# First batch of a retention and Fourier-mixing kernel: k transposed straight from f32 on TensorE, its decay moved into the masked eviction, loads and weight issues reordered

## The chip, the cores and the metric

The kernel runs on one core of one Trainium2 chip. The metric is the device time of one execution in microseconds (us). Before the change it is 247.43 us, the median of three runs (247.37 to 247.91). The profiled execution has a span of 246.0 us. Engines are named as in the profile: PE is TensorE (PEld its weight loads), DVE is VectorE, ACT is ScalarE, POOL is GpSimd, SP is SyncE, whose queue issues the loads and stores.

## The reference

Inputs are q, k and v of shape [4 batches, 8 heads, 768 positions, 64], and two weight matrices of 512 x 2048 and 2048 x 512, all f32. The first part is retention with a decay gamma for each head, gamma = 1 - 2^(-5-h). For each position t it updates a 64 x 64 state and reads it out:

```
state = gamma * state + outer(k[t], v[t])
y[t]  = (1/8) * q[t] @ state
```

The eight heads side by side give x of shape [4, 768, 512]. The second part adds to x the real part of its two-dimensional Fourier transform over positions and channels (u), normalises each row of u to mean 0 and variance 1 (un), and returns

```
u + relu(un @ w_ch1) @ w_ch2
```

## The kernel before

**Tiling of the retention.** A batch's 768 positions are cut into 6 chunks of 128 (NCH), its 8 heads into 4 pairs, taken in the order 0, 1, 3, 2 (PAIR_ORDER). Inside a chunk the sum over earlier positions is a matrix product: scores k q^T, masked to the causal triangle and weighted with powers of gamma, times v. Across chunks a state is carried. For a pair the kernel makes:

- q16: q cast to f16 (q0_unit, L388, on Pool), and kd: k cast to f16 and multiplied with gamma^(127-p), p being the position in the chunk (k0_unit, L396, on Pool; for the last pair the second head is on ScalarE, L408).
- qT and kT: both transposed on TensorE, six 128x128 transposes each (t0_unit, L424), through a PSUM tile that ScalarE copies to SBUF (te_unit, L436). Since kT comes from kd, the decay of k is already in the scores.
- the scores of the two heads, 12 small matmuls (am_unit, L447), which VectorE multiplies with the causal mask and with the constant gamma^(-128) while it moves them out of PSUM to atm (ae_unit, L462). This is the masked eviction. Four of them make a pair.
- the state product kd^T v of five chunks (kv0_unit, L471, needs kd and v16) and the scan over chunks on VectorE (sc_unit, L484), which reads the factors of gamma^128 from gk5. gk5 is filled per pair by gk_unit (L223) on ScalarE, from gk2.
- y: the state read with q (yx_unit, L509) and atm times v (yi_unit, L495), moved to x by ScalarE with the factor gamma^(p+1)/8 (x0_unit, L525).

**The Fourier part and the layer.** Tables of sines and cosines are worked out on the chip at the start (trig_dve, L277, on VectorE; t_act, L308, on ScalarE); x is folded (fold_s, fold_d on VectorE) and multiplied with them (s1_unit, s2_unit). The two layers are the matmuls of L930, L947 and L973, which fill TensorE from about 40 us to the end.

**Order of the work.** The first batch is written out by hand in first_units (L1031): a list of units, each of which emits a few instructions. After each unit pin() fixes the order on every engine, so that an engine takes its instructions in the order of this list. Between the units stand fillers (L142): 128x512 matmuls of zeros that only keep TensorE at work, six of them before the first unit, then four, three, one and so on. From the second batch on, units are spread by due times in several streams (emit).

**Loads.** The loads of the first batch are issued at the start on SP's queue, in the order q, k, v of pair 0, then of pair 1 and so on, 384 KB each (load_unit, L152); k's load takes both heads of the pair. The weights come later in eight pieces of 512 KB from Pool's queue (w1_unit, w2_unit): w1_unit(0) stands in the list just after the cast of pair 3's q, the other seven after the cast of its v.

**PSUM.** The transposes, the scores and the state product share a pool of five banks (ps_g), given out in turn.

Of the kernel before, what the change touches and what calls it, by code (L numbers as in the profile page):

```python
# [11 lines left out]
AF = mybir.ActivationFunctionType  # L12
# [6 lines left out]
P = 128  # L19
# [18 lines left out]
def kernel(  # L38
# [113 lines left out]
    def load_unit(b, i, after=None):  # L152
        def run():
            h0 = 2 * PAIR_ORDER[i]
            for name, src in srcs.items():
# [3 lines left out]
                dma = nc.sync.dma_start(t, src[b, h0:h0 + 2].rearrange(rows, p=P))  # L159
# [21 lines left out]
    gexp = const.tile([P, 2, H], f32, tag="gexp")  # L181
    gq8, gkd = gexp[:, 0], gexp[:, 1]
    ident16 = const.tile([P, P], f16, tag="ident16")
    tmp = up.tile([P, NCH, DM], f32, tag="u32", name="tmp")
# [13 lines left out]
    for h in range(H):  # L198
# [6 lines left out]
                            op0=ALU.mult)  # L205
    nc.scalar.activation(gexp, gexp, AF.Exp, bias=0.0, scale=1.0)
# [4 lines left out]
    make_identity(nc, ident16)  # L211
    nc.gpsimd.affine_select(out=maskf, in_=maskf, compare_op=ALU.is_ge, fill=0.0, base=0,
# [10 lines left out]
    def gk_unit(hp):  # L223
        def run():
            nc.scalar.copy(gk5[:, hp, :, 1:], gk2[:, hp:hp + 1].unsqueeze(1).to_broadcast(
                [P, D, NCH - 2]))
        return run
# [168 lines left out]
    def k0_unit(i):  # L396
        def run():
            h0 = 2 * PAIR_ORDER[i]
            k32 = in_of.pop(("k", 0, i))
            kd = kd_of[0, i] = kp.tile([P, NCH, 2, D], f16, tag="kd16", name="kd16")  # L400
            nc.gpsimd.tensor_scalar(out=kd[:, :, 0, :], in0=k32[:, 0], scalar1=gkd[:, h0:h0 + 1],
                                    scalar2=1.0, op0=ALU.mult, op1=ALU.mult)
            if i < 3:
                nc.gpsimd.tensor_scalar(out=kd[:, :, 1, :], in0=k32[:, 1],
                                        scalar1=gkd[:, h0 + 1:h0 + 2], scalar2=1.0,
                                        op0=ALU.mult, op1=ALU.mult)
            else:
                nc.scalar.activation(kd[:, :, 1, :], k32[:, 1], AF.Copy, bias=0.0,  # L408
                                     scale=gkd[:, h0 + 1:h0 + 2])
        return run  # L410
# [13 lines left out]
    def t0_unit(i, part):  # L424
        def run():
            if part == 0:
                at[0, i] = dict(kT=tp.tile([P, NCH, P], f16, tag="kT", name="kT"),
                                qT=qts[i % 2][:, 0])
            src = (q16_of, kd_of)[part][0, i]
            tq = at[0, i]["tq", part] = ps_g.tile([P, NCH, P], f16, tag="g", name="tq",  # L430
                                                  padded_shape=[P, 8, P])
            for c in range(NCH):
                nc.tensor.transpose(tq[:, c, :], src[:, c].rearrange("p a b -> p (a b)"), ident16)
        return run

    def te_unit(i, part):  # L436
        def run():
            st = at[0, i]
            tq = st["tq", part]
            if part == 0:  # L440
                nc.scalar.copy(st["qT"].rearrange("p c t -> p (c t)").rearrange(
                    "p (t c) -> p t c", c=NCH), tq.rearrange("p c t -> p t c"))
            else:
                nc.scalar.copy(st["kT"], tq)
        return run
# [16 lines left out]
    def ae_unit(i, half, h2):  # L462
        def run():
# [3 lines left out]
                scalar=float(gam[2 * PAIR_ORDER[i] + h2] ** (-P)),  # L467
# [516 lines left out]
    def w1_unit(g):  # L984
        def run():
            f0 = g * (DFF // 4)
            w_dma.append(nc.gpsimd.dma_start(
                w116[:, :, f0:f0 + DFF // 4],
                moe_w_ch1[:, f0:f0 + DFF // 4].rearrange("(cb p) f -> p cb f", p=P)))
        return run  # L990
# [40 lines left out]
    def first_units():  # L1031
# [10 lines left out]
        def x(i):  # L1042
# [5 lines left out]
        un = [ts_dve(0), gk_unit(o[0]), gk_unit(o[1]), t_act(0, 0), t_act(0, 1),  # L1048
              q0_unit(0), t0_unit(0, 0), filler(4), ts_dve(1), te_unit(0, 0), t_act(0, 2),
              k0_unit(0), t0_unit(0, 1), filler(3), te_unit(0, 1), ts_dve(2), td_dve(0), t_act(1, 0),  # L1050
              t_act(1, 1), t_act(1, 2), v0_unit(0)]
        un += a(0) + [filler(1), kv0_unit(0)] + e(0, *std) + [sc_unit(0)]
        un += [q0_unit(1), t0_unit(1, 0), te_unit(1, 0), t_act(2, 0), t_act(2, 1), filler(4),
               k0_unit(1), t0_unit(1, 1), te_unit(1, 1)]
# [3 lines left out]
        un += [q0_unit(2), t0_unit(2, 0), te_unit(2, 0), csn_unit(1), filler(3), k0_unit(2),  # L1058
               t0_unit(2, 1), te_unit(2, 1)]
        un += y(1) + [td_dve(1), yx_unit(1), filler(2)] + x(1) + [  # L1060
            gk_unit(o[2]), t_act(3, 0), t_act(3, 1), v0_unit(2)]
        un += a(2) + [filler(1), kv0_unit(2)] + e(2, *std) + [sc_unit(2), t_act(3, 2),
                                                              csn_unit(2)]
        un += [q0_unit(3), w1_unit(0), t0_unit(3, 0), te_unit(3, 0), filler(3)] + y(2)
        un += [fold_s(0, 0, 258, 0, 1), g0_unit(0, (0,)), k0_unit(3), t0_unit(3, 1),
               te_unit(3, 1), yx_unit(2), gk_unit(o[3]), x0_unit(2, 0), x0_unit(2, 1),
               t_act(4, 0), t_act(4, 1), filler(2), v0_unit(3)]
        un += [w1_unit(g) for g in range(1, 4)] + [w2_unit(g) for g in range(4)]
        un += a(3) + e(3, (0, 0), (1, 0)) + [kv0_unit(3), filler(4), sc_unit(3), t_act(4, 2)]
# [108 lines left out]
```

## Time and profile before

Busy time of the whole span and of the first 30 us, from the profile:

| engine | busy in the span, us | 0 to 10 us | 10 to 20 us | 20 to 30 us |
|---|---|---|---|---|
| PE | 234.4 (95%) | 7.31 | 8.66 | 7.98 |
| DVE | 177.5 (72%) | 8.77 | 9.36 | 8.94 |
| ACT | 124.3 (51%) | 8.14 | 8.85 | 7.34 |
| POOL | 81.3 (33%) | 7.11 | 5.59 | 8.39 |

A row of a timeline gives the start and the duration in us, then the engine, the line, the operation, what is written and read, the shape and the number of instructions; in brackets stands how long the engine was idle before it and what ended that. Rows merge neighbours, so that the duration of "x6" is that of all six together. A row of the waits gives the total in us, how often, and the longest. In a table by stretches each engine has its busy time and the number of its instructions.

The loads of the first batch land, from issue and time to landing, at 4.2, 6.0 and 7.7 us (q, k, v of pair 0), 8.9, 10.7, 12.4 (pair 1), 13.4, 15.3, 17.0 (pair 2) and 19.6, 21.3, 22.6 us (pair 3).

### The profile page before, as it was taken

The page shows a single profiled execution, that of the slowest core. Times are in us where ns is not written, and L with a number is a line of the kernel's source. Part 1 is how long each engine was busy: PE and PEld are TensorE (multiplying, and loading weights), DVE is VectorE, ACT ScalarE, POOL GpSimd, SP SyncE. Part 2 cuts the span into 40 slices and gives each one's busy share as a digit, 9 for nine tenths or more (in the row PEclk, how much of TensorE's full clock was granted, in tenths as well). Part 3 has the DMA queues.
Part 4 walks back from the last instruction along what each step waited for, and adds up shares of the span by engine and source line. Part 5 has one row for each costly group of instructions (what it writes and reads, how often), then busy time and mean ns, then how long its engine had stood idle before and what let it go on. Part 6 is the DMA issues. An engine that isn't in the chain of part 4 may idle for free.

```text
span 246.0 us, 5309 instructions
## 1 busy us (share of the span) xinstructions
PE 234.4 (95%) x2024; PEld 144.4 (59%) x2024; DVE 177.5 (72%) x430; ACT 124.3 (51%) x276; POOL 81.3 (33%) x146
## 2 busy tenths in 40 slices
PE   6897899999999999999999999999999998999994
PEld 2454668956676655665567446665666455445543
DVE  8998957898788788995987648887895657424122
ACT  8798669477785445742247415732257217202500
POOL 6667600376500068690001637660003214000000
PEclk9999999999999999999999999999999999999999
DMA  8998999699999287988999589596100331121012
GB/s 174 257 260 138 200 204 206 152 250 261 275 233 214 56 171 176 190 174 149 242 266 210 119 183 181 108 138 150 58 0 3 60 133 30 38 85 43 0 45 85
DMA packets 99209, 36.39 MB, mean 148 GB/s; under 512 B 89840, under 2 KB 96240, under 8 KB 99184
## 3 DMA queue, kind: packets, MB, share of 16 engines
q1 hardware_dynamic: 94960, 31.86, 62.5%
q0 software_dynamic: 4224, 4.19, 10.5%
q8 instruction: 16, 0.26, 0.5%
q14 instruction: 9, 0.07, 0.1%
HBM read 27.26 MB, written 6.29 MB: 136 GB/s over the span
## 4 chain that ended last, share of the span: by engine, by line
PE 72%; DVE 8%; POOL 7%; ACT 4%; SPq 3%; DMA 2%; issue 2%; POOLq 0%; DVEq 0%
PE psc L973 30%; PE psh L930 23%; SPq L159 3%; PE ps L730 3%; PE psh L947 3%; PE wkA L594 3%; DMA k<-in_k_dram 2%; PE wkY L648 2%; POOL u L864 2%; POOL u L866 2%; PE wkY L644 1%; DVE bst L883 1%; PE wkK L613 1%; DVE u L834 1%; PE pq L827 1%
## 5 line engine op out<-in xcount | busy, mean ns | idle before, releaser
L973 PE MATMUL psc<-w,ht 128*128 128x512 f16 (+1 forms) x400 | 89.6, 370 | 0.1
L930 PE MATMUL psh<-unT,w 128*128 128x384 f16 x448 | 81.3, 326 | 0.6 <-ACT ht L934 0.6
L973 PEld LDWEIGHTS <-ht 128*128 128x128 f16 x400 | 38.1, 98 | 35.5 <-issue 0.3
L930 PEld LDWEIGHTS <-w 128*128 128x128 f16 x448 | 42.3, 98 | 24.9 <-issue 1.3
L934 ACT ACTIVATE ht<-psh 128x384 f16<-128x384 f32 x64 | 30.6, 488 | 39.4 <-PE psh L930 38.3
L864 POOL TENSOR_TENSOR u<-u,x 128x256 f32<-128x256 f32 x21 | 13.3, 634 | 102.3 <-DVE u L834 90.7
L977 DVE SCALAR_TENSOR_TENSOR ob<-psc,stats,u 128x512 f32<-128x512 f32 (+1 forms) x25 | 18.1, 722 | 27.4 <-PE psc L973 27.3
L936 DVE TENSOR_SCALAR ht<-psh 128x384 f16<-128x384 f32 x48 | 26.3, 551 | 8.6 <-PE psh L930 8.3
L597 DVE TENSOR_TENSOR atm<-wkA,maskp 128x512 f16<-128x512 f32 x36 | 23.9, 685 | 1.0 <-PE wkA L594 1.0
L885 ACT ACTIVATE un<-u,stats 128x512 f16<-128x512 f32 x21 | 15.1, 721 | 16.9 <-DVE stats L884 8.7
L883 DVE BATCH_NORM_STATS2 bst<-u 128x6 f32<-128x512 f32 x21 | 14.6, 694 | 9.7 <-POOL u L866 9.5
L623 DVE SCALAR_TENSOR_TENSOR s<-s,gk,wkK 128x128 f16<-128x128 f16 x48 | 16.4, 343 | 2.3 <-ACT s L619 1.4
L656 ACT ACTIVATE x<-wkY,gexp 128x384 f16<-128x384 f32 x24 | 12.8, 580 | 9.3 <-PE wkY L648 9.3
L145 PE MATMUL wps<-ht 128*128 128x512 f16 x40 | 13.3, 439 | 2.2 <-POOL ht L196 2.2
L377 POOL TENSOR_SCALAR kd<-k,gexp 128x384 f16<-128x384 f32 x24 | 13.8, 584 | 2.4 <-DMA k<-in_k_dram 2.4
L866 POOL TENSOR_TENSOR u<-u,x 128x256 f32<-128x256 f32 x21 | 13.3, 634 | 2.8 <-DVE u L837 1.5
L594 PE MATMUL wkA<-qTz,kT 128*128 128x256 f16 x72 | 13.6, 273 | 0.0
L829 ACT COPY qn<-pq 128x128 f32<-128x128 f32 x18 | 4.9, 274 | 14.1 <-PE pq L827 13.9
L947 PE MATMUL psh<-unT,w 128*128 128x128 f16 x192 | 11.5, 219 | 0.1
L947 PEld LDWEIGHTS <-w 128*128 128x128 f16 x192 | 11.0, 98 | 0.7 <-issue 0.5
L382 POOL TENSOR_SCALAR v<-v 128x768 f16<-128x768 f32 x12 | 10.0, 830 | 2.0 <-DMA v<-in_v_dram 1.9
L594 PEld LDWEIGHTS <-kT 128*128 128x128 f16 x72 | 6.9, 98 | 6.0 <-DVE s L623 0.4
(164 smaller groups left out, 318.2 us busy)
## 6 DMA issues: line engine op xcount, KB each, us to landing
q<-in_q_dram SPq DMA_DIRECT2D x16, 384.0 KB, 6.2
k<-in_k_dram SPq DMA_DIRECT2D x16, 384.0 KB, 5.6
v<-in_v_dram SPq DMA_DIRECT2D x16, 384.0 KB, 6.6
out_dram<-ob SPq DMA_DIRECT2D x23, 256.0 KB, 2.6
w<-in_moe_w_ch_dram POOLq DMA_DIRECT2D x8, 512.0 KB, 11.1
out_dram<-ob SPq DMA_DIRECT2D x2, 128.0 KB, 1.7
unT<-un SPq DMA_TRANSPOSE x15, 2.4
qTz<-q16z SPq DMA_TRANSPOSE x8, 3.8
```

Of the source, the lines that this page charges most:

```text
L594: mm = nc.tensor.matmul(wk[:, c2], st["kT"][:, c, :], st["qT"][:, :, c, :], start=True, stop=True)
L597: nc.vector.tensor_tensor(out=st["atm"][:, 2 * part:2 * part + 2], in0=wk, in1=maskp[:, PAIR_ORDER[i]].unsqueeze(1).to_broadcast([P, 2, 2, ...
L623: nc.vector.scalar_tensor_tensor(out=s16[:, c], in0=s16[:, c - 1], scalar=gk2[:, hp:hp + 1], in1=wk[:, c - c0], op0=ALU.mult, op1=ALU.add)
L864: nc.gpsimd.tensor_tensor(out=u[:, kb, 0:256], in0=u[:, kb, 0:256], in1=x[:, kb, 0, 1:257], op=ALU.add)
L866: nc.gpsimd.tensor_tensor(out=u[:, kb, 256:512], in0=u[:, kb, 256:512], in1=x[:, kb, 1, 257:1:-1], op=ALU.add)
L883: nc.vector.bn_stats(bst, u[:, kb, :])
L930: nc.tensor.matmul(psh, w116[:, cb, fb * P:(fb + 1) * P], unT[:, cb, rt * 384:(rt + 1) * 384], start=(cb == 0), stop=(cb == 3))
L934: nc.scalar.activation(ht16[:, fb, :], psh, AF.Relu, bias=0.0, scale=-1.0)
L936: nc.vector.tensor_scalar(out=ht16[:, fb, :], in0=psh, scalar1=-1.0, scalar2=0.0, op0=ALU.mult, op1=ALU.max)
L947: mm = nc.tensor.matmul(psh[:, f], w116[:, cb, fb * P:(fb + 1) * P], unT[:, cb, kb * P:(kb + 1) * P], start=(cb == 0), stop=(cb == 3))
L973: nc.tensor.matmul(psc[:, c0:c1], ht16[:, fb, rb3 * P:(rb3 + 1) * P], w216[:, fb, c0:c1], start=(fb == 0), stop=(fb == NFB - 1))
L977: nc.vector.scalar_tensor_tensor(out=ob[:, c0:c1], in0=psc[:, c0:c1], scalar=lb[b]["st"][:, rb, 3:4], in1=lb[b]["u"][:, rb, c0:c1], op0=AL ...
```

## The change

kT of the first batch is no longer made from kd. TensorE transposes the f32 tile of k itself (with an f32 identity, ident32, made on Pool from the f16 one), in two halves of three chunks with a PSUM bank each, and ScalarE copies each half to f16. The transposes thereby need only k's load and not Pool's cast. Since the decay is then missing from the scores, the masked eviction multiplies with gks = gamma^-(p+1), one value per partition, in place of the constant gamma^(-128); gks is one more row of the table gexp. For the transposes both heads of a chunk must lie side by side, so the tile of k is laid out by chunk, head and channel, and k's load is split into one for each head. kd is still made, for the state product alone, for all pairs on Pool.

With it, the four copies of gk5 go from ScalarE to Pool, ahead of the first cast of q. w1_unit(0) and w1_unit(1) both stand after the units of pair 3's q and ahead of its k cast, and the first waits for the last of the transposes of that q. The units x0_unit(2, ...) and t_act(4, ...) stand later in the list, behind pair 3's first two masked evictions.

The diff, cut to its core:

```diff
-                dma = nc.sync.dma_start(t, src[b, h0:h0 + 2].rearrange(rows, p=P))
+                flat = src[b, h0:h0 + 2].rearrange(rows, p=P)
+                if b == 0 and name == "k":
+                    t = t.rearrange("p h c d -> p (h c d)").rearrange("p (c h d) -> p c h d",
+                                                                      c=NCH, h=2)
+                    for h2 in range(2):
+                        dma = nc.sync.dma_start(t[:, :, h2], flat[:, h2])
+                else:
+                    dma = nc.sync.dma_start(t, flat)
...
+    nc.vector.tensor_scalar(out=gexp[:, 2], in0=lgrow, scalar1=icol[:, 3:4], scalar2=-1.0,
+                            op0=ALU.mult, op1=ALU.mult)
...
     make_identity(nc, ident16)
+    nc.gpsimd.tensor_copy(ident32, ident16)
...
-            nc.scalar.copy(gk5[:, hp, :, 1:], gk2[:, hp:hp + 1].unsqueeze(1).to_broadcast(
+            nc.gpsimd.tensor_copy(gk5[:, hp, :, 1:], gk2[:, hp:hp + 1].unsqueeze(1).to_broadcast(
...
-            if i < 3:
-                nc.gpsimd.tensor_scalar(out=kd[:, :, 1, :], in0=k32[:, 1],
-                                        scalar1=gkd[:, h0 + 1:h0 + 2], scalar2=1.0,
-                                        op0=ALU.mult, op1=ALU.mult)
-            else:
-                nc.scalar.activation(kd[:, :, 1, :], k32[:, 1], AF.Copy, bias=0.0,
-                                     scale=gkd[:, h0 + 1:h0 + 2])
+            nc.gpsimd.tensor_scalar(out=kd[:, :, 1, :], in0=k32[:, :, 1],
+                                    scalar1=gkd[:, h0 + 1:h0 + 2], scalar2=1.0,
+                                    op0=ALU.mult, op1=ALU.mult)
...
+            k32 = in_of["k", 0, i]
+            tk = at[0, i]["tk", half] = ps_g.tile([P, 3, P], f32, tag="g", name="tk",
+                                                  padded_shape=[P, 4, P])
+            for c3 in range(3):
+                nc.tensor.transpose(tk[:, c3, :], k32[:, 3 * half + c3].rearrange(
+                    "p a b -> p (a b)"), ident32)
...
-                nc.scalar.copy(st["kT"], tq)
+                nc.scalar.copy(st["kT"][:, 3 * half:3 * half + 3], st["tk", half])
...
-                scalar=float(gam[2 * PAIR_ORDER[i] + h2] ** (-P)),
+                scalar=gks[:, 2 * PAIR_ORDER[i] + h2:2 * PAIR_ORDER[i] + h2 + 1],
...
+            if g == 0:
+                tc.add_manual_dep(w_dma[0].ins, at[0, 3]["tr"].ins.name,
+                                  mybir.DependencyInfo(mybir.DependencyClass.Sync,
+                                                       mybir.DependencyReason.DATA),
+                                  reason="weights behind the loads")
...
-        un = [ts_dve(0), gk_unit(o[0]), gk_unit(o[1]), t_act(0, 0), t_act(0, 1),
-              q0_unit(0), t0_unit(0, 0), filler(4), ts_dve(1), te_unit(0, 0), t_act(0, 2),
-              k0_unit(0), t0_unit(0, 1), filler(3), te_unit(0, 1), ts_dve(2), td_dve(0), t_act(1, 0),
-              t_act(1, 1), t_act(1, 2), v0_unit(0)]
+        def tq(i):
+            return [q0_unit(i), t0_unit(i, 0), te_unit(i, 0)]
+
+        def tk(i):
+            return [t0_unit(i, 1, 0), te_unit(i, 1, 0), t0_unit(i, 1, 1), te_unit(i, 1, 1)]
+
+        un = [ts_dve(0), gk_unit(o[0]), gk_unit(o[1]), gk_unit(o[2]), gk_unit(o[3]), t_act(0, 0),
+              t_act(0, 1)] + tq(0)
+        un += [filler(4), ts_dve(1), t_act(0, 2), k0_unit(0)] + tk(0)
+        un += [filler(3), ts_dve(2), td_dve(0), t_act(1, 0), t_act(1, 1), t_act(1, 2), v0_unit(0)]
...
-        un += [q0_unit(3), w1_unit(0), t0_unit(3, 0), te_unit(3, 0), filler(3)] + y(2)
-        un += [fold_s(0, 0, 258, 0, 1), g0_unit(0, (0,)), k0_unit(3), t0_unit(3, 1),
-               te_unit(3, 1), yx_unit(2), gk_unit(o[3]), x0_unit(2, 0), x0_unit(2, 1),
-               t_act(4, 0), t_act(4, 1), filler(2), v0_unit(3)]
-        un += [w1_unit(g) for g in range(1, 4)] + [w2_unit(g) for g in range(4)]
-        un += a(3) + e(3, (0, 0), (1, 0)) + [kv0_unit(3), filler(4), sc_unit(3), t_act(4, 2)]
+        un += tq(3) + [w1_unit(0), w1_unit(1), filler(3)] + y(2)
+        un += [fold_s(0, 0, 258, 0, 1), g0_unit(0, (0,)), k0_unit(3)] + tk(3)
+        un += [yx_unit(2), filler(2), v0_unit(3)]
+        un += [w1_unit(g) for g in range(2, 4)] + [w2_unit(g) for g in range(4)]
+        un += a(3) + e(3, (0, 0), (1, 0)) + [x0_unit(2, 0), x0_unit(2, 1), t_act(4, 0),
+                                            t_act(4, 1), kv0_unit(3), filler(4), sc_unit(3),
+                                            t_act(4, 2)]
```

## Prediction

> **What bounds the kernel now.** I read the shares by engine first. TensorE is busy for 95% of the span, so from some point on the kernel is a stream of matmuls and only a stretch before that point can be shortened. The busy time by stretches finds it: TensorE is full from about 40 us, while the first 30 us are not TensorE's.
>
> ```profile
> core 0: us, PE busy (x) PEld busy (x) DVE busy (x) ACT busy (x) POOL busy (x), PEclk, DMA share, GB/s
> ...
> 10.00:20.00 10.00, 8.66 (x131) 5.11 (x125) 9.36 (x23) 8.85 (x17) 5.59 (x10) 1.00 1.27 252
> 20.00:30.00 10.00, 7.98 (x114) 5.21 (x114) 8.94 (x21) 7.34 (x16) 8.39 (x11) 1.00 0.99 159
> ...
> 100.00:150.00 50.00, 50.00 (x402) 30.45 (x401) 37.90 (x90) 21.44 (x51) 15.31 (x26) 1.00 1.00 186
> ```
>
> The reader is to see 9.36 of 10 us on VectorE between 10 and 20 us, more than on any other engine, and TensorE's 8.66 of which much is filler. A shift of the first batch moves all that follows by the same amount; nothing in it is shortened otherwise. The waits of VectorE from 9 to 31 us are one line, 1.4 us in three waits:
>
> ```profile
> DVE atm L465 <- PE wkA L458: 1.4, 3, 0.9
> ```
>
> So in these 20 us VectorE works through its fixed order with 1.4 us of slack: 0.25 us before pair 1's masked evictions, 0.18 before pair 2's, 0.92 before pair 3's. The last is what the change can collect. The timeline shows the work in front of it:
>
> ```profile
> 19.69 0.83 POOL L392 TENSOR_SCALAR q16z<-q 128x768 f16<-128x768 f32 x1 [1.76 <-PE wkK L480]
> ...
> 20.46 0.96 POOL L987 DMA_DIRECT2D w<-in_moe_w_ch_dram  x1
> ...
> 21.47 1.29 POOL L401 TENSOR_SCALAR kd<-k,gexp 128x384 f16<-128x384 f32 x1
> ...
> 22.81 0.34 PEld L433 LDWEIGHTS <-kd 128*128 128x128 f16 x6 [0.85 <-POOL kd L401]
> ...
> 23.36 0.80 ACT L444 COPY kT<-tq 128x768 f16<-128x768 f16 x1 [0.92 <-PE tq L433]
> ...
> 24.62 1.02 DVE L465 SCALAR_TENSOR_TENSOR atm<-wkA,maskf 128x384 f16<-128x384 f32 x2 [0.92 <-PE wkA L458]
> ```
>
> Pair 3's k lands at 21.3 us (issued 14.47, 6.8 to landing); its cast on Pool, the transposes and the eviction of kT put the masked eviction at 24.62, though VectorE was free at 23.70. The start of pair 0 is the other place to read:
>
> ```profile
> 4.30 0.83 POOL L392 TENSOR_SCALAR q16z<-q 128x768 f16<-128x768 f32 x1 [0.18 <-DMA q<-in_q_dram]
> ...
> 5.18 0.82 PE L433 MATMUL tq<-ident,q16z 128*128 128x128 f16 x6 [0.29 <-POOL q16z L392]
> ...
> 5.80 1.74 PE L145 MATMUL wps<-ht 128*128 128x512 f16 x4
> ...
> 7.49 0.51 PE L433 MATMUL tq<-ident,kd 128*128 128x128 f16 x6
> ...
> 7.84 0.81 PE L145 MATMUL wps<-ht 128*128 128x512 f16 x3
> ...
> 9.99 1.94 DVE L465 SCALAR_TENSOR_TENSOR atm<-wkA,maskf 128x384 f16<-128x384 f32 x4
> ```
>
> Four fillers in 1.74 us are 0.43 each; from about 7.5 us on, three in 0.81 are 0.21 apart (the rest is drain): TensorE runs at half speed until then. The first masked eviction waits for nothing, VectorE being at the tables until 10.06.
>
> **What the skill says.** "TensorE: Matmul & The Clock Gate", Part 1: the HAM clock gate: the array runs at half clock until a free-running window of some 3.4 us has been busy. The trace agrees: work from 5.18 us almost without a gap, full pace at 7.5. The same page, LDWEIGHTS and weight-path perf modes: a load of 128 columns takes 128/1.2 = 107 ns, and the fast load isn't there for FP32; the f16 transposes here stand 57 ns apart (six loads in 0.34 us). Its table of terms says that transpose mode is four times as fast for FP32; "FP8 and Floating Point Precision", TensorE Precision Notes, gives true FP32 four passes. No f32 transpose is in this trace. "GPSIMD Engine Reference", Key points: it shares its SBUF interfaces with VectorE. The trace agrees: L284 takes 0.36 us at 2.93 and 0.97 at 4.37, under a cast on Pool.
>
> **The change, part by part.**
>
> *Pool at the start.* Added ahead of q's first cast: the f32 identity (0.30, the 128x128 row of L345) and the four copies of gk, which were on ScalarE. A copy has 256 elements per partition; between L345 (128 elements, 0.30) and L401 (384, 0.58) lies 0.44. Bounds: 0.30 and 0.56 (the memset of gk, also 256 strided elements). I take 0.43 with overlap, four are 1.7. Pool's setup ends at 4.12, so the cast of q runs 6.1 to 6.95 in place of 4.30 to 5.13: **+1.8 us**. Queued behind it on TensorE are all of pair 0's transposes and fillers.
>
> *TensorE, pair 0.* It now idles from 4.89 to 7.0, so the window that had opened the clock by 7.5 is mostly idle, and the clock likely opens only about 11. Before, q's transposes and four fillers took 5.18 to 7.49, 2.3 us at half speed; after, 7.0 to 9.3. Six f32 transposes: lower bound 0.057 each (as f16), upper 0.228 (four passes). I take 0.12, the slow weight load with a little more, since loads overlap matmuls here; at half clock 0.24, six are 1.45: 10.75. Three fillers at full clock, 0.65: 11.4, when both halves of kT are out too (0.49 each, the 128x384 f16<-f32 row of L934). The scores start at 11.45, the first masked eviction 0.37 later (as 13.78 to 14.15): 11.8 instead of 9.99, **+1.8 us**.
>
> *Pairs 1 and 2.* Six transposes cost 6 x (0.12 - 0.057) = 0.4 us more. TensorE was busy for 3.69 of pair 1's 4.15 us and 4.11 of pair 2's 4.63; with 0.4 more, and the 0.25 and 0.18 us of VectorE's slack there, pair 1 grows by about 0.1 and pair 2 stays: **+0.1**. kT's eviction in two halves costs ScalarE 0.17 us a pair (0.87 for 0.69), against 0.4 us for each gk copy taken away: nothing, as no one waits for ScalarE there but kT itself. A per-partition scalar in the masked eviction is the same pass over 384 elements: nothing. The longer exponent table (24 columns for 16): nothing, under the loads.
>
> *Pair 3.* The transposes wait for k's landing (21.3) and no longer for the cast, so the gap of 0.92 us closes: **-0.9**. The two weight loads now wait for q's last transposes (21.1 before) and take 0.96 + 0.77 on Pool; behind them are both halves of k's cast (0.58 each) and half of v's (0.50), which the state product and then the scan need. Without the shift at the start this gives 21.1 + 1.7 + 1.2 + 0.5 + 0.5 = 25.0 for the scan, against 25.56 now, so Pool caps any gain at 0.6 us; with the shift the scan comes after 26 and Pool is hidden. The weights have slack: the last part of the first matrix lands by 33, its first use is at 34.86.
>
> *k's loads by head.* The same 256-byte pieces; two issues of 0.45 us instead of one, where the queue otherwise stalls 1.5 to 2.7 us on q and v: nothing.
>
> Sum: 1.8 + 0.1 - 0.9 = **+1.0 us, 248.4**.
>
> **Rivals.**
> *The clock opens in time* (a window happens to fall on the six fillers at the start and stays open, or the gk copies are as short as 0.30). Then transposes and fillers take 1.2 us after 7.0, f32 transposes 0.72, fillers 0.65: scores at 9.6, and VectorE is not late. The gain is the gap, capped by Pool at 0.6: **246.8**. For it: VectorE's 0.92 us gap is plain in the trace, and pair 0's cast has almost 3 us until VectorE wants it. Against: 2.1 us without TensorE work just where the clock was won.
> *It cancels*: the clock opens between (about 9.3), or a transpose takes 0.2 at full clock, so that 0.5 to 1.2 us are lost at the start and the gap gives them back: **247.5**.
> *Four passes at half clock*: 0.46 each, six are 2.7 us, pairs 1 and 2 become TensorE-bound by 0.5 us each: 1.8 + 1.3 + 1.0 - 0.9 - 0.8 (what VectorE's order and later pairs overlap) = +2.4: **249.8**. Against: the page's line on transpose mode.
>
> **How the numbers follow.** Late clock with cheap transposes 0.40, four passes 0.08, cancelled 0.22, clock in time 0.30. Slower by more than 0.5 us: 0.40 + 0.08 = 0.48; within: 0.22; faster: 0.30. The range runs from the gain's cap, 246.7, to just under the four-pass case, 249.6.
>
> **What would show it.** Right: in the changed kernel the first cast of q starts near 6.1; fillers at 0.43 us still after 9 us; the first masked eviction near 11.8; pair 3's masked eviction with no wait ahead of it, starting near 25.7; everything after it later by the same amount. Wrong: f32 transposes near 0.06 or 0.23 us apart; fillers at 0.21 before 8 us; Pool's gk copies far from 0.43; the scan of pair 3 waiting for the state product; TensorE waiting for weights after 34 us.

## The result, and the profile after

The changed kernel takes 250.68 us (median of 4 runs, 250.59 to 251.07) against 247.67 us (247.37 to 248.12) for the kernel before on the same chip: ratio 1.0124, 95% interval 1.0108 to 1.0139, or +3.0 us. The forecast was +1.0. In the profiled execution TensorE's granted clock fell for some microseconds near 30 us (mean 0.993; 1.0 in the other three, whose spans are 248.8 us instead of 249.3).

First, where the time isn't. The first-layer matmuls of the first batch start at 38.08 us instead of 35.15, +2.93. From there to the last masked eviction of the later batches both kernels take the same: 178.00 - 38.08 = 139.92, and 175.07 - 35.15 = 139.92. So the whole loss lies ahead of 38 us, as the prediction assumed it would.

The two stretches, after, in the columns of the table of before (TensorE, weight loads, VectorE, ScalarE, Pool, clock, DMA):

```profile
10.00:20.00 10.00, 7.85 (x114) 5.60 (x113) 9.40 (x22) 7.56 (x15) 6.59 (x11) 1.00 1.26 252
20.00:30.00 10.00, 8.33 (x110) 4.85 (x109) 9.57 (x19) 6.55 (x15) 7.46 (x11) 0.94 0.75 119
```

VectorE is busier than before (9.40 for 9.36, 9.57 for 8.94), not less held up. Its waits for the scores did shrink, in total, count and longest:

```profile
DVE atm L479 <- PE wkA L472: 0.7, 2, 0.4
```

That is 0.7 us for the 1.4 of before, and pair 3's wait of 0.92 is gone. So the change got what it was for, and VectorE paid for it elsewhere. The start of the changed kernel, by the timelines of VectorE, Pool and TensorE:

```profile
1.24 1.01 DVE L209 CAST icol<-icol_i 128x6 f32<-128x6 int32 x1
...
2.02 0.20 POOL masks.py:197 MEMSET ident<- 128x128 f16 x1
...
2.13 2.74 PE L145 MATMUL wps<-ht 128*128 128x512 f16 x6 [2.13 <-POOL ht L204]
...
3.12 0.95 DVE L232 CAST tmp<-tmp 128x386 f32<-128x386 int32 x1
...
3.81 2.14 POOL L236 COPY gk<-gk 128x256 f32<-128x256 f32 x4
...
5.92 0.92 POOL L403 TENSOR_SCALAR q16z<-q 128x768 f16<-128x768 f32 x1
...
6.90 0.51 PE L439 MATMUL tq<-ident,q16z 128*128 128x128 f16 x6 [2.02 <-POOL q16z L403]
...
7.24 1.03 PE L145 MATMUL wps<-ht 128*128 128x512 f16 x4
...
8.11 0.82 PE L447 MATMUL tk<-ident,k 128*128 128x128 f32 x6
...
9.51 0.51 PE L472 MATMUL wkA<-qTz,kT 64*128 64x128 f16 x12
...
12.20 2.19 DVE L479 SCALAR_TENSOR_TENSOR atm<-wkA,gexp,maskf 128x384 f16<-128x384 f32 x4
```

The scores are multiplied at 9.51, but the masked eviction starts only at 12.20, with no wait behind it: VectorE was at its tables until then. TensorE begins at half speed (the six fillers at 2.13 are 0.43 us apart) and is at full speed at 6.90 (the fillers at 7.24 are 0.21 apart); this document says that its clock opens. Here it opened between 4.87 and 6.90, while TensorE idled. The record of the granted clock reads 1.00 in this first phase too and shows only later falls.

The same place in the kernel before, with its fold and its first layer, which are taken up further down:

```profile
1.23 0.40 DVE L201 CAST icol<-icol_i 128x6 f32<-128x6 int32 x1
...
2.04 0.54 POOL masks.py:197 MEMSET ident<- 128x128 f16 x1
...
2.08 0.36 DVE L221 CAST tmp<-tmp 128x386 f32<-128x386 int32 x1
...
21.38 1.01 DVE L673 TENSOR_TENSOR xab<-x 128x774 f16<-128x774 f16 x2
...
35.15 3.00 PE L947 MATMUL psh<-unT,w 128*128 128x128 f16 x48
```

The same instructions on the same operands: before, VectorE's cast of icol took 0.40 and was over at 1.63, and Pool's memset of the identity, which met VectorE's next instructions, took 0.54; after, the cast takes 1.01, past the end of that memset, and the memset 0.20. The two engines change places as to who waits, and VectorE's next cast takes 0.95 for 0.36. Its first table instruction starts at 4.11 us instead of 2.47, so that 1.64 of the 2.21 us by which the first eviction is late are lost before the tables begin.

The Trainium skill ("SBUF — State Buffer", Who interferes with whom) says that VectorE and GpSimd share a port pair, which VectorE uses in a two-port mode, and of which it uses the reading side when an instruction has two SBUF inputs; the one that issues first holds the pair for its whole instruction while the other blocks. The traces agree that one of the two waits: a 0.40 us cast that comes out at 1.01 has waited for about the length of a neighbour (0.52, the memset of ht from 1.56 to 2.08). That this cast runs in a two-port mode is not shown by any run.

The fold in that list is the fold of pairs 0 to 2. In the changed kernel it comes out like this:

```profile
22.50 1.73 POOL L1001 DMA_DIRECT2D w<-in_moe_w_ch_dram  x2 [3.19 <-PE tq L439]
...
23.72 2.11 DVE L687 TENSOR_TENSOR xab<-x 128x774 f16<-128x774 f16 x2
...
24.26 0.59 POOL L412 TENSOR_SCALAR kd<-k,gexp 128x384 f16<-128x384 f32 x1
...
26.86 1.13 DVE L479 SCALAR_TENSOR_TENSOR atm<-wkA,gexp,maskf 128x384 f16<-128x384 f32 x2
...
38.08 3.00 PE L961 MATMUL psh<-unT,w 128*128 128x128 f16 x48
```

Before, the fold took 1.01 and the cast of k beside it 1.29 (shown in the prediction; alone it takes 0.58). After, the cast takes 0.59 and the fold 2.11. The operations on the fold's tile give the shortest, median and longest of its two instructions in ns:

```profile
L687 DVE TENSOR_TENSOR xab<-x x2: 535/1098/1661, 23.7 to 24.2; 128x774 f16<-128x774 f16 x2
```

The first has its usual length; the second, recorded from 24.17 to 25.83, spans both casts of k (24.26 to 25.42). Its 1.66 us are about its own 0.54 and both casts (0.59 and 0.58) together, so it seems to have waited for two instructions of Pool. Its record starts before theirs, so the record that starts first isn't always the winner's.

VectorE's order in both kernels, from the starts of its masked evictions, accounts for the 2.93 us:

| stretch | before | after | difference |
|---|---|---|---|
| start to pair 0's first eviction | 9.99 | 12.20 | +2.21 |
| pair 0 to pair 1 | 4.16 | 4.34 | +0.18 |
| pair 1 to pair 2 | 4.63 | 4.34 | -0.29 |
| pair 2 to pair 3 | 5.84 | 5.98 | +0.14 |
| pair 3 to the first layer's matmuls | 10.53 | 11.22 | +0.69 |

Inside the rows: each pair's four evictions grow by 0.24 or 0.25. Between pairs 1 and 2 the table entries are 0.65 shorter (1.20 for 1.85), meeting fewer of Pool's instructions. Between pairs 2 and 3 stand the fold's +1.10 and the closed gap's -0.92. In the last row some 0.5 is the fall of the clock (a span of 249.3 us against 248.8).

### The profile page after: what moved, and what is told of

It reads as the page before. It is cut to its first block, busy times and chain, and to the rows that moved or that the text cites. A ratio compares the mean times of both kernels' runs of the same rounds, so it can differ in the third digit from the quotient of the medians.

```text
span 249.3 us, 5322 instructions
## 1 busy us (share of the span) xinstructions
PE 235.2 (94%) x2024; PEld 146.8 (59%) x2024; DVE 180.8 (73%) x431; ACT 122.9 (49%) x275; POOL 84.3 (34%) x152
## 4 chain that ended last, share of the span: by engine, by line
PE 74%; DVE 13%; POOL 5%; ACT 4%; issue 2%; DVEq 0%; POOLq 0%
PE psc L987 29%; PE psh L944 24%; PE ps L744 3%; PE psh L961 3%; PE wkA L608 3%; PE wkY L662 2%; POOL u L880 2%; PE wps L145 2%; DVE atm L479 1%; PE wkY L658 1%; DVE bst L897 1%; DVE xab L687 1%; PE wkK L627 1%; DVE tmp L295 1%; POOL u L878 1%
## 5 line engine op out<-in xcount | busy, mean ns | idle before, releaser
L608 PE MATMUL wkA<-qTz,kT 128*128 128x256 f16 x72 | 13.6, 273 | 0.0
```

Source lines behind the costliest of these rows:

```text
L608: mm = nc.tensor.matmul(wk[:, c2], st["kT"][:, c, :], st["qT"][:, :, c, :], start=True, stop=True)
```

## The experiments

Each difference is from the median of the kernel before that was timed beside it on the same chip (247.84, 247.55, 247.65 and 247.90 us on the four chips). A mean clock is that of one execution, granted to TensorE over the whole span.

**1. The pointer taken out.** From the changed kernel, with the constant back in the eviction and without the row of gks and the VectorE instruction that fills it. The decay is left out of the first batch's scores.

```diff
-    nc.vector.tensor_scalar(out=gexp[:, 2], in0=lgrow, scalar1=icol[:, 3:4], scalar2=-1.0,
-                            op0=ALU.mult, op1=ALU.mult)
...
-                scalar=gks[:, 2 * PAIR_ORDER[i] + h2:2 * PAIR_ORDER[i] + h2 + 1],
+                scalar=float(gam[2 * PAIR_ORDER[i] + h2] ** (-P)),
```

> The changed kernel with the constant gamma^(-128) in the masked eviction and without the table row gks and the VectorE instruction that starts it. The decay of k is thereby left out of the first batch's scores. Theory 2 (a scalar read per partition makes each of the sixteen masked evictions 0.06 us longer, and VectorE is what bounds this stretch): 0.547 us each again, 1.0 us less, and up to 0.2 for the instruction left out, so 249.5. Rival (VectorE's order has slack for it): 250.4 to 250.7.

248.99 us (248.93 to 249.56), ratio 1.0056 (1.0044 to 1.0068): +1.15 for the +3.0 of the whole change. The group of masked evictions in the kernel before and in the changed kernel (busy us, mean ns, wait before):

```profile
L465 DVE SCALAR_TENSOR_TENSOR atm<-wkA,maskf 128x384 f16<-128x384 f32 x16 | 7.9, 547 | 1.4 <-PE wkA L458 1.4
...
L479 DVE SCALAR_TENSOR_TENSOR atm<-wkA,gexp,maskf 128x384 f16<-128x384 f32 x16 | 8.8, 608 | 0.7 <-PE wkA L472 0.7
```

and in this kernel:

```profile
L477 DVE SCALAR_TENSOR_TENSOR atm<-wkA,maskf 128x384 f16<-128x384 f32 x16 | 7.8, 544 | 0.8 <-PE wkA L470 0.8
```

64 ns each, sixteen times: 1.0 us, all on the engine that sets the pace. More comes back than that, since in this trace the fold, now starting at 23.06, took 1.04 us: the cast of k beside it starts only at 23.84 and is the one that gets longer (0.71). Of the single edits this one gives most back.

TensorE's clock opened late in this execution: after 2.23 us of idling q's transposes took 0.82 us (0.51 in the changed kernel) and the scores started at 11.37. Still the first eviction, at 11.94, waited for nothing, because VectorE was at its tables until then.

**2. The pointer alone, put into the kernel before.** gamma^-128 is read from an added row instead of a constant; nothing else differs.

```diff
+    nc.vector.tensor_scalar(out=gexp[:, 2], in0=lgrow, scalar1=-float(P), scalar2=None,
+                            op0=ALU.mult)
...
-                scalar=float(gam[2 * PAIR_ORDER[i] + h2] ** (-P)),
+                scalar=gks[:, 2 * PAIR_ORDER[i] + h2:2 * PAIR_ORDER[i] + h2 + 1],
```

> The kernel before with the same factor gamma^(-128) in the masked eviction, but read per partition from one more row of the table of exponents, as the change does it. Theory 2: each of the sixteen takes 0.608 us instead of 0.547, so 1.0 us more on VectorE less the 0.4 us of slack at pairs 1 and 2, and what the added row costs at the start: 248.4 to 249.5. Rival (hidden in VectorE's waits): 247.7 to 248.1.

248.28 us (248.1 to 248.67), ratio 1.0029 (1.0018 to 1.004): +0.73. The evictions are again 608 ns each, so the added length is the instruction's own and not a matter of the transposes or of Pool. The first starts at 10.60 (9.99 before), behind the added VectorE instruction of the new row; how much of the 0.73 is due to it and how much to the longer evictions, this run can't tell. The waits absorb part of both: 0.7 us are left of 1.4.

**3. The gk copies.** Back on ScalarE at their old places in the changed kernel, and alone on Pool in the kernel before.

```diff
-            nc.gpsimd.tensor_copy(gk5[:, hp, :, 1:], gk2[:, hp:hp + 1].unsqueeze(1).to_broadcast(
+            nc.scalar.copy(gk5[:, hp, :, 1:], gk2[:, hp:hp + 1].unsqueeze(1).to_broadcast(
```

> The changed kernel with the four gk copies back on ScalarE, at their old places in the list; all else stays changed. Theory 1 (the copies hold the SBUF interfaces that GpSimd and VectorE share, and VectorE's tables at the start come late): the tables end 0.6 to 1.4 us earlier than 12.2 us, and the time falls from 250.7 to 249.3 to 250.1. Rival (the late start of TensorE and its f32 transposes set the first masked eviction): with the cast of q 2 us earlier, TensorE starts 2 us earlier and the whole of the 2 us comes back, 248.7; if neither is on the path, 250.7.

250.92 us (249.98 to 252.45), ratio 1.0132 (1.0104 to 1.0159): +3.1, by the median nothing is won back. But four of the six executions have a mean clock of 0.986 to 0.993 (in the trace it is 0.50 from 28.6 to 32.0 us). The two at full clock took 249.98 and 250.02, where the changed kernel at full clock takes 250.59 to 250.74. By these two, the copies give back 0.6 to 0.8 us, which the clock hides in the median. The first eviction starts at 11.87 (12.20 with the copies on Pool), and icol's cast still takes 1.01.

> The kernel before with its four gk copies on Pool ahead of the first cast of q, as the change has them. Theory of the prediction (Pool's delay of the first cast by 1.8 us is what makes the first masked eviction late): first masked eviction 1 to 2 us later, 248.2 to 249.5. Rival (VectorE is busy with its tables until 10 us anyway and ScalarE gains): 247.3 to 248.0.

248.55 us (248.25 to 249.25), ratio 1.0034 (1.0021 to 1.0047): +1.0. Here the cast takes 1.01 as well and the first eviction starts at 12.11, 2.12 late; by the layers' start (36.45) 1.30 of it is left in that execution. The clock opens late, on the course that the prediction described: three fillers at 10.07 take 1.49 us. The copies alone suffice to turn the start over; they aren't needed for it.

**4. The other additions of the start, without their use.** Into the kernel before: the added row and the f32 identity on Pool together, and then the identity alone.

```diff
+    nc.vector.tensor_scalar(out=gexp[:, 2], in0=lgrow, scalar1=-float(P), scalar2=None,
+                            op0=ALU.mult)
...
     make_identity(nc, ident16)
+    nc.gpsimd.tensor_copy(ident32, ident16)
```

> The kernel before with the two additions of the change to the start alone, neither of them used: one more row in the table of exponents (a VectorE instruction and 24 columns instead of 16) and the f32 identity copied on Pool. Theory 4 (small additions at the start shift VectorE against Pool and its tables then run into Pool's casts): the first masked eviction comes 1 us or more later than 9.99, time 248.2 to 249.5. Rival (0.15 us of VectorE and 0.29 of Pool are hidden): 247.7 to 248.0.

249.37 us (248.44 to 249.63), ratio 1.0066 (1.0052 to 1.0081): +1.8. The first eviction starts at 11.53. VectorE then waits 1.95 us for pair 1's scores: TensorE had idled 1.76 us until a PSUM bank came free, and the four fillers behind that took 1.91 us instead of 1.03; the granted clock is 0.50 from 12.0 to 15.4 us. Five of the six executions have a mean clock of 0.992 or 0.993; the one at 0.998 took 248.44, +0.9.

> The kernel before with one thing added: the copy of the identity to float32 on Pool, which nothing reads. It is the half of the start of the change that no run has had alone. If the added Pool pass is what sends VectorE's tables later, the cast of icol takes about 1.0 us and the first masked eviction starts 1 to 1.5 us later than 9.99: 248.2 to 249.0. Rival: Pool's 0.30 us only moves Pool's own queue, the tables end as before, and the time is 247.5 to 247.9.

248.39 us (248.12 to 249.88), ratio 1.003 (1.0018 to 1.0043): +0.49. The added copy takes 0.31 us on Pool at 2.65, and yet the cast that starts at 1.24 already takes 1.01, with the memset of the f16 identity at 0.20:

```profile
1.24 1.01 DVE L202 CAST icol<-icol_i 128x6 f32<-128x6 int32 x1
```

The first eviction starts at 11.20. Later slack takes most of that up: the profiled execution's layer matmuls start at 35.30, 0.15 late.

**5. When the cast starts.** Two tiny memsets ahead of it on VectorE, in the kernel before.

```diff
     nc.vector.memset(maskf, 1.0)
+    for h in range(2):
+        nc.vector.memset(last[:, h:h + 1], 0.0)
     nc.vector.tensor_copy(icol[:, 0:6], icol_i[:, 0:6])
```

> The kernel before with two more tiny memsets on VectorE ahead of the cast of icol, so that this cast starts some tenths of a microsecond later. If the cast's 1.01 us in the kernel after comes from when it meets Pool's memset and not from what it computes, the cast takes about 1.0 us here too, VectorE's tables end 0.5 to 1 us later, and the time is 248.0 to 248.6. Rival: the slack ahead of the first pairs takes the delay up, 247.5 to 247.9, or the cast stays at 0.40 us.

247.65 us (247.55 to 247.97), ratio 0.9999 (0.9991 to 1.0007): no difference; the cast takes 0.40. In the trace it still starts at 1.23, as before: the edit didn't move it, so this run says nothing of what a later start would do. What decides whether the cast or Pool's next instruction gets its turn first stays open. The start time on record is no guide: 1.23 with 0.40 and 1.24 with 1.01 differ by a hundredth, and the first kernel of experiment 8 had 1.01 from 1.23. Only this is shown, with one trace for each kernel: in the eight kernels with Pool copies added behind it the cast took 1.01, and in the five others that have it on VectorE (before, the pointer alone, this one and the two of experiment 9) it took 0.40.

**6. icol's cast moved to Pool**, in the changed kernel, so that VectorE can't lose there.

```diff
+    nc.gpsimd.tensor_copy(icol[:, 0:6], icol_i[:, 0:6])
     nc.gpsimd.iota(kf_i, pattern=[[1, KN]], base=0, channel_multiplier=0)
...
-    nc.vector.tensor_copy(icol[:, 0:6], icol_i[:, 0:6])
```

> The changed kernel with the conversion of the index columns to f32 (0.40 us on VectorE before, 1.01 in the changed kernel and in each variant of it so far) moved to Pool, behind the three index instructions. Theory 4 (VectorE loses 0.6 us to Pool's memset there, which pushes its table work into Pool's later work, where it loses more): the tables start 0.6 to 1.0 us earlier than 4.11 us, and the first masked eviction comes at 10.5 to 11.5 us instead of 12.2, time 249.3 to 250.2. Rival (the lateness is made later, by the casts and gk copies alone): the first masked eviction stays near 12, 250.6.

251.3 us, ratio 1.0104 (1.0059 to 1.0148), in two groups: twice 248.4, and 251.09 to 252.5. The profile is of the second group. VectorE's tables end at 9.74, 2.5 us earlier, but now Pool has the cast and loses time: its setup and the gk copies end at 7.18 instead of 5.95, and TensorE starts late:

```profile
8.34 0.82 PE L439 MATMUL tq<-ident,q16z 128*128 128x128 f16 x6 [3.18 <-POOL q16z L403]
8.95 1.91 PE L145 MATMUL wps<-ht 128*128 128x512 f16 x4
10.66 1.03 PE L447 MATMUL tk<-ident,k 128*128 128x128 f32 x6
```

After 3.18 us of idling the fillers take 1.91 (1.03 in the changed kernel, after 2.02). The clock wasn't lost over the idle time, since the six fillers ahead of it had run at half speed as well (2.74 us); it opened late. The first eviction starts at 12.74, behind a wait of 3.01: now VectorE doesn't cover TensorE's late start. From the first layer (38.18) to the last masked eviction this execution takes the usual 139.92 us, so what it loses is lost at the start.

**7. TensorE kept at work there.** The kernel of 6 with 15 fillers instead of 6 in the first group.

> The kernel after, with the cast of icol on Pool as before in the last experiment, and fifteen idle-time matmuls in the first group instead of six, so that TensorE stays at work until q's transposes. If the two groups of times of that experiment (248.4 and about 251.5) come from TensorE's clock having closed while it was idle from 5.2 to 8.3 us, all times now lie near 248.4 and the first masked eviction starts near 10.5 to 11.3. Rival: the two groups come from something else (the order in which Pool and VectorE get their turns) and both are still there.

251.55 us (251.27 to 252.51), ratio 1.0158 (1.0138 to 1.0178). The clock was open in time: the four fillers at 8.68 take 1.03, the first eviction starts at 11.42, the first layer at 36.80, only 1.65 us after that of the kernel before. But between there and the last masked eviction it takes 141.44 us, where before and after take 139.92. Of these 1.5 us, 1.15 are a wait in the second batch, for a DMA transpose of kT that came late (in the kernel before nothing waits there):

```profile
116.09 0.39 PE L608 MATMUL wkA<-qTz,kT 128*128 128x256 f16 x2 [1.15 <-DMA kT<-kd]
```

The start went as the theory of the clock says; the time did not. By the start of the first layer the clock is worth 1.4 us (38.18 in 6, 36.80 here), and the groups of 6 lie 2.9 us apart (spans of 249.4 and 246.5). Its fast group has no trace, so where the rest lies stays open.

**8. Both the pointer and the gk copies undone**, and separately the last pair's cast of k given back to ScalarE, each in the changed kernel. The first leaves the decay out of the first batch's scores, as 1 does; its edits are those of 1 and 3. The second is this:

```diff
+            if i < 3:
+                nc.gpsimd.tensor_scalar(out=kd[:, :, 1, :], in0=k32[:, :, 1], ...)
+            else:
+                nc.scalar.activation(kd[:, :, 1, :], k32[:, :, 1], AF.Copy, bias=0.0,
+                                     scale=gkd[:, h0 + 1:h0 + 2])
```

> Both edits together, the decay of k left out of the first batch's scores. If the two costs lie one after the other on VectorE they add: 248.3 to 249.1. If they hide behind one another, no faster than the faster of the two alone.

250.02 us (248.53 to 250.41), ratio 1.0078 (1.0053 to 1.0103): more than with the pointer alone undone. The trace shows why: TensorE idled 2.01 us for a PSUM bank, went back to work, and 1.1 us later its granted clock fell to 0.50, from 13.6 to 17.1 us.

```profile
12.54 0.49 PE L437 MATMUL tq<-ident,q16z 128*128 128x128 f16 x6 [2.01 <-DVE atm L477]
...
12.88 1.15 PE L145 MATMUL wps<-ht 128*128 128x512 f16 x4
...
13.82 1.49 PE L445 MATMUL tk<-ident,k 128*128 128x128 f32 x6
```

The six f32 transposes take 1.49 us instead of 0.82, and VectorE waits 1.83 us for pair 1's scores. The two executions at full clock took 248.53 and 248.59, as expected of costs that add; the other four have a mean clock of 0.992 or 0.993. An edit that frees one engine left another idle, and it lost its clock. The length of the idle time doesn't decide that: in the next kernel TensorE idles 2.01 us at the same place and keeps its clock (four fillers in 1.03 us).

> The changed kernel with the second half of pair 3's k cast back on ScalarE. Theory 3 (Pool's casts of pair 3 run into the fold of x on VectorE, whose two instructions take 2.1 us in place of 1.0): the fold falls to 1.0 to 1.6 us and the time to 249.6 to 250.2. Rival (the fold is slowed by the first half too, or the half on ScalarE delays x): 250.4 to 250.9.

250.28 us (250.16 to 250.82), ratio 1.0111 (1.0096 to 1.0126): +2.4, some 0.6 less than the change. The fold and what meets it:

```profile
23.59 1.28 DVE L691 TENSOR_TENSOR xab<-x 128x774 f16<-128x774 f16 x2
...
24.13 1.10 POOL L412 TENSOR_SCALAR kd<-k,gexp 128x384 f16<-128x384 f32 x1
```

1.28 for 2.11. The one remaining cast of 384 elements takes 1.10 instead of 0.58: now it is Pool that waits.

**9. The idea without its costs.** From the kernel before: k is transposed from f32 as in the change, but the decay moves from k to v. The state product needs the factor on one of the two, and so does the product of scores and v. The eviction keeps its constant; the identity is copied on ScalarE, and the gk copies and weights stay as they were. The whole reference is computed.

```diff
+            nc.gpsimd.tensor_scalar(out=kd, in0=k32, scalar1=1.0, scalar2=1.0, op0=ALU.mult,
+                                    op1=ALU.mult)
...
+            for h2 in range(2):
+                last_cast[0, i] = (nc.vector if i == 3 and h2 else nc.gpsimd).tensor_scalar(
+                    out=v16[:, :, h2, :], in0=v32[:, :, h2, :],
+                    scalar1=gkd[:, h0 + h2:h0 + h2 + 1], scalar2=1.0, op0=ALU.mult, op1=ALU.mult)
...
+        nc.scalar.copy(ident32, ident16)
```

> The kernel before with k transposed from float32 as in the change, but with the decay moved from k to v: v is cast with gamma^(127-p) per row and k is cast plainly, so that the masked eviction keeps its constant scalar and no row is added to the exponentials; the gk copies and the weights stay where they were in the kernel before, and ident32 is made on ScalarE. The whole reference is computed. If the change's loss comes from the pointer scalar and from Pool's and VectorE's start, and its idea is sound, the 0.92 us gap of the last pair closes without the losses: 246.9 to 247.4, under the kernel before. Rival: the three float32 transposes per half and the two PSUM evictions per pair, or the added ScalarE copy at the start, cost what the gap gives: 247.5 to 248.5.

247.80 us (247.35 to 248.17), ratio 1.0001 (0.9993 to 1.0009). The loss is gone, and the gap of pair 3 too, but the time is that of before. VectorE's waits for scores add up to 2.1 us:

```profile
DVE atm L475 <- PE wkA L468: 2.1, 2, 1.5
```

They have moved ahead: pair 0's eviction starts 0.82 earlier (9.17), but pair 1's masked eviction comes no sooner than before (14.24, before 14.15). By the trace Pool holds it: the cast of v, now in two halves with a factor each, takes 1.42 us for 0.83, so that pair 1's q is cast from 9.67 on instead of 8.96, and from its transposes (10.56) to these scores TensorE works without a gap. No run tried to change that. Pair 3's eviction starts at 24.41 for 24.62, without a wait: VectorE itself is the limit there.

Then the last pair set in another order: the second head of v on ScalarE, and that cast ahead of the copies to x in the list, the scores ahead of two fillers.

```diff
+                if i == 3 and h2:
+                    nc.scalar.activation(v16[:, :, h2, :], v32[:, :, h2, :], AF.Copy, bias=0.0,
+                                         scale=gkd[:, h0 + h2:h0 + h2 + 1])
+                    continue
...
-        un += a(3) + e(3, (0, 0), (1, 0)) + [kv0_unit(3), filler(4), sc_unit(3), t_act(4, 2)]
+        un += a(3) + [filler(2)] + e(3, (0, 0), (1, 0)) + [kv0_unit(3), filler(4), sc_unit(3),
+                                                           t_act(4, 2)]
```

> The kernel with the decay moved from k to v, with the last pair set in another order: the second head of v is cast on ScalarE instead of VectorE (0.71 us there), and the scores are multiplied ahead of the two idle-time matmuls (0.60 us) instead of behind them. The whole reference is computed. If the last pair's masked eviction is held by VectorE's 0.71 us and by those matmuls, it starts 0.6 to 0.8 us earlier than the 24.41 of the kernel with the decay on v, and the time is 246.9 to 247.3, under the kernel before. Rival: ScalarE is delayed by its added cast (the copies of the outputs and the tables stand behind it) and hands the gain back: 247.5 to 248.0.

247.25 us (246.98 to 247.92) against 247.90, ratio 0.9975 (0.9963 to 0.9987): 0.65 us less than the kernel before.

```profile
23.55 1.01 DVE L479 SCALAR_TENSOR_TENSOR atm<-wkA,maskf 128x384 f16<-128x384 f32 x2
...
34.08 3.00 PE L961 MATMUL psh<-unT,w 128*128 128x128 f16 x48
```

Pair 3 starts 0.86 us earlier than in the kernel above it, and the layers at 34.08 instead of 35.15 before. The kernel before with only the last pair reordered was not run, so how the 0.65 us divide between the idea and the order is not shown. In its trace the last pair's scores, at 24.25, waited for the copy of kT, which ended at 24.16; the fillers alone didn't hold them.

## Why the prediction was wrong

The side was right (slower) and the size was not: 250.68 us lies above the range, whose upper end was 249.6. Three steps failed, all of them on VectorE: what Pool's work at the start does to its tables (+2.2 us, where +1.8 had been put down to TensorE), the pointer scalar (put at nothing, +1.0) and the fold beside Pool's casts (not in the sum, +1.1). In numbers the last two make the miss of 2.0 us; the first had the wrong cause.

**What bounds the kernel: right.** VectorE's order, and a shift that is carried unchanged to the end (139.92 us in both).

**Pool at the start: right in kind.** q's cast was put at 6.1 to 6.95; it ran 5.92 to 6.84. The gk copies take 0.535 each, not 0.43, and nearer to the upper bound; Pool's setup ahead of them ended earlier than before because its memset and selection didn't lose to VectorE.

**TensorE, pair 0: near in size, wrong in cause.** The first masked eviction was put at 11.8 and came at 12.20; that they lie so close is luck. "The clock likely opens only about 11" failed in the profiled execution: the six fillers at 2.13 still ran at half speed (0.43 each), and after the idle time of 2.02 us q's transposes ran at full speed at once (0.51 us for six, 0.82 before), so the clock opened while TensorE idled. In two kernels with the same start, those of experiment 1 and of the second run of 3, it did open late, after 2.23 us of idling. The skill's window ("TensorE: Matmul & The Clock Gate", Part 1) runs free of the work; the step let it begin with the work at 5.18 and left out the six fillers from 2.15 on. The traces agree with that: in four of them the clock falls later on, for 3.4 us each time, the length that the page gives the window, and a whole number of such lengths before the fall lies a moment that fits the opening: in the changed kernel it falls at 28.8, and seven lengths earlier is 4.93, in the idle time; where both additions of experiment 4 are made it falls at 12.0, and two earlier is 5.12; in the first runs of 3 and 8 it falls at 28.6 and 13.6, and six and two earlier are 8.14 and 6.81, amid work whose pace changes there. The page has it that the window doesn't start with the kernel; the forecast could not know where it lay, and took one side.

**VectorE at the start: the first failed step.** The step took VectorE as unchanged and let TensorE alone set the first eviction. VectorE's tables ended at 12.28 instead of 10.06, through instructions that came out longer beside Pool's work at the start, and every copy added on Pool turned that start over, down to the one that nothing reads (experiment 4: first eviction at 11.20 for 9.99). The contention had been quoted as a fact of the skill with its number in this trace, 0.36 to 0.97, and then left out of the sum: +2.2 us without a term of its own. A late clock would not have come on top, since the later of the two engines counts: in experiment 1 the scores started at 11.37 and VectorE was ready for them only at 11.94. The transposes' own price was right: 0.82 us for six, with loads 0.13 apart, for 0.12.

**"A per-partition scalar in the masked eviction is the same pass over 384 elements: nothing": the second failed step.** It costs 61 ns an instruction (547 to 608), sixteen times +1.0 us, and experiments 1 and 2 show this length from both sides. The skill ("DVE: scalar operands, raw-bit mode, write accounting and state across instructions", Scalar operands) says that such a scalar is read per partition and doesn't take up the second tensor stream. Nothing in these runs speaks against that, yet the instruction got longer. A shape that the trace of before didn't have was given the price zero instead of bounds. VectorE being the pace-setter, this is the worst place for it.

**Pairs 1 and 2: +0.1 forecast; -0.11 measured** (+0.18 and -0.29), with the evictions' +0.5 hidden in it against -0.65 from a table stretch with less contention.

**Pair 3: the gap closed as forecast, the gain didn't come: the third failed step.** The wait of 0.92 is gone and pair 3's eviction starts without one. But the stretch as a whole grew by 0.14, since the fold of 1.01 became 2.11 beside the casts of k that the new order puts there. The step looked at Pool only as a queue ("Pool caps any gain at 0.6 us") and not as a neighbour on VectorE's ports. Experiment 8 takes 0.83 us of the fold's growth away by moving one cast.

**The sum.** Forecast 1.8 + 0.1 - 0.9 = +1.0. Measured 2.2 (start) + 1.0 (pointer) + 1.1 (fold) - 0.65 (tables between pairs) - 0.7 (waits, the closed gap among them) = 2.95. The fall of the clock in the profiled execution adds 0.5, and shorter small instructions around the fold and in pair 0 take as much away. The parts don't add up one by one when tried alone (pointer +0.73, identity +0.49, gk copies +1.0), because slack absorbs some of each and a late TensorE adds to others.

**What stays open:** what decides which of the two engines gets its turn first at 1.2 to 2.0 us; what makes the two groups of times of experiment 6 beyond the late clock; and what the moved weight loads, x0_unit and t_act do alone, which no run tried. The split loads of k are in both kernels of experiment 9 too, which lose nothing to the kernel before.

## What to carry to other kernels

On a stretch where VectorE sets the pace, each instruction added on Pool is to be priced twice: by its place in Pool's queue, and by the VectorE instructions that run beside it, which came out longer by 0.6 to 1.1 us each here, or not at all. A change of operand kind in a repeated eviction is not free until a row with that operand shows it: 61 ns, sixteen times, was a third of this loss. And before a gap is booked as gain, see what the new order places next to the long instructions around it; the same idea with the factor moved to v, where a pass over the data existed anyway, broke even, and won 0.65 us once the last pair's work was reordered and part of it given to ScalarE. Where the clock falls in some executions and not in others, compare the executions at full clock too, not the medians alone.

## What was not expected of the hardware

- Two engines at the same few instructions can settle them in different ways: VectorE's cast in 0.40 us and Pool's memset in 0.54, or 1.01 and 0.20 (0.40 and 0.30 with the pointer alone). An unrelated copy on Pool, more than a microsecond later in its order, went with the change from one to the other.
- A pointer scalar adds 61 ns to a VectorE eviction of 128x384 from PSUM.
- TensorE's clock was kept over 2.12 us of idling in one kernel and lost over 1.76 in another. In the changed kernel it fell at 28.8 us though no idle time in the 3.4 us before was longer than 0.73; TensorE was busy for 1.8 us of these.
- f32 transposes of 128x128 stand 0.13 us apart at full clock, against 0.057 for f16.
